# Attention, then a gated network, on one core: 25 instead of 22 visits with both products with V in one block, and a first Strassen pair that no longer waits for the last mask

## The chip, the core and the metric

The kernel runs on one core of a Trainium2 chip. The metric is the time of one execution on the device in microseconds (us), median of three runs. In the texts PE is the matrix engine, DVE the vector engine, ACT the scalar engine, POOL the general engine (GpSimd) and SP the engine that issues the DMAs.

## The reference

Attention over 8 batches, 8 heads, 576 tokens, head size 64, with all scores dropped that lie more than tau = 0.02 under the row's greatest; then a gated network over the 4608 tokens.

```python
scores = scale * q @ k.T                      # (8, 8, 576, 576)
scores = where(scores >= max(scores) - tau, scores, -1e9)
attn = softmax(scores)
x = (attn @ v) as (4608, 512)
out = (sigmoid(x @ w_gate) * (x @ w_val)) @ w_out   # 512 -> 1536 -> 512
```

## The kernel before

**Attention** goes through 32 visits, one for each batch b (0 to 7) and each pair of heads hp (0 to 3); a visit's tiles carry b and hp in their names (`av7_3_0` is of visit (7,3)). A visit has nine tiles of 128 query rows by 576 keys: four for each head, and one (`l`) that holds the 64 left over queries of both. For each tile PE makes scores (`s`, line 669, or 661 in the first four visits), DVE their maximum (676), ACT the exponential (690), DVE the mask with the row sum (693), PE four transposes of the result (`tp`, 770) and one of its left over keys (`lk`, 783), and ACT copies them (`pt`, `pl`). The products with V (`av`, 808) follow for both heads together: each head fills 64 columns of the array, and the two heads stand on different halves of the output's partitions. Two banks of results come of a visit, one for the queries of tiles 0 and 1 and one for tiles 2 and 3 with the left over ones. In an unpaired visit these are two blocks on PE, each placed as soon as its tiles are there. In a paired visit (`PAIRED`) one operation issues both, 68 matmuls in a row. ACT moves both banks to `xf`, POOL multiplies by the reciprocal row sums, which go through DRAM (`rd`, `rb`), and a DMA or a split puts the block away.

**The network** runs over nine blocks of 512 tokens (the ninth gathers the left over ones). Blocks 0 to 2 take three matmuls for each product (high and low halves), as `m` (888), `o` (939) and, for the output of blocks 1 and 2, seven products of a Strassen scheme (`pairp`, 1227). Blocks (3,4), (5,6) and (7,8) go as Strassen pairs: seven products for each piece of the weights, summed in three banks a, b and c (`qa`, `qb`, `qc`, line 1138; then `ra`, `rb`, `rc`, 1284). Bank b lies in a score slot (tag `s`), of which there are two once the network has begun. The operands of the first pair (`xs0_p1` to `xs0_p3`) were put away in DRAM earlier and are loaded into buffers that the attention gives back (`kd`, `k2`, `p`, `vs`, `x`), 512 KB each.

**What sets the order:** a planner goes through all operations with estimated costs, keys and limits on buffers, and fixes one order for each engine. Attention has keys by its tile count, the network's PE work has keys from 1e6 on, so attention goes first wherever it can and the network fills what it leaves. Operations that were ready in the plan but not on the chip hold up what stands behind them on their engine. `masked` is a one-element list: it holds the mask operation that was written last, and at the place where the Strassen pairs are written that is the one of the last tile of visit (7,3). All products of the first pair (`k` = 0) wait for it.

Of the kernel before, what the change touches and what calls it, by code (L numbers as in the profile page):

```python
# [10 lines left out]
F32 = mybir.dt.float32  # L11
F32R = mybir.dt.float32r
I32 = mybir.dt.int32
AF = mybir.ActivationFunctionType
ALU = mybir.AluOpType
# [28 lines left out]
class Plan:  # L44
# [10 lines left out]
    def buf(self, tag, shape, dtype, name, cls=None):  # L55
        return Buf(self, tag, shape, dtype, name, cls)
# [185 lines left out]

NPS = 4

AV_COST, AV_PAIR = 0.0096, 5.25


def PAIRED(b, hp):
    return b >= 3 or b == 2 and hp % 2


def THR(t):
# [59 lines left out]
def act(n):  # L312
    return 0.19 + 0.0008 * n
# [10 lines left out]
def mm(n):  # L324
    return 0.014 + 0.000418 * n
# [3 lines left out]
def kernel(  # L329
# [25 lines left out]
    nc = tc.nc  # L355

    B, NPAIR, _, P, SK = k.shape
# [8 lines left out]
    SM = NJ * P  # L366
# [19 lines left out]
    zero_t = cp.tile([P, 1], F32, tag="zero", name="zero_t")  # L386
# [9 lines left out]
    scale_t = cp.tile([P, 1], F32, tag="scale", name="scale_t")  # L396
# [4 lines left out]
    ps_more = ahead.enter_context(tc.tile_pool(name="ps_more", bufs=1, space=PSUM))  # L401
# [9 lines left out]
    active = {"att": 1, "moe": 0}  # L411

    class Both(Plan):
        def cap(self, tag, cls):
            if tag == "s" and active["moe"]:
                return 2 if cls is None else None
            if tag != "b":
                return None
            if cls == "conv":
                return 1  # L420
            if cls == "att":
                return 2 if active["moe"] else 3
            return 2 if active["att"] else 4
# [19 lines left out]
            if o is last_att[0]:  # L443
                active["att"] = 0

    last_att, first_late, masked, more = [None], [None], [None], [ps_more]
    plan = Both(pools, slots)
    op, buf = plan.op, plan.buf

# [92 lines left out]
    class Visit:  # L542
# [66 lines left out]
        def plain_scores(self, key, n):  # L609

            pair = 4 * self.b + self.hp
# [13 lines left out]
                    ), writes=parts)  # L625
            for h in range(2):
                for j, (c0, c1) in enumerate(pieces if h == 0 else [(0, S)]):
                    op("ACT", act(c1 - c0), key + h, lambda h=h, c0=c0, c1=c1: nc.scalar.activation(
                        qn.ap[:, h, c0:c1], qn.ap[:, h, c0:c1], AF.Copy, scale=scale_t[:, 0:1]
                    ), writes=[(qn, (h, y)) for y in ((j,) if len(pieces) > 1 and h == 0 else (0, 1))])  # L630

    def tile_steps(vis, g, i, key):

# [50 lines left out]
        else:  # L684
# [5 lines left out]
        op("ACT", 0.74, key, lambda: nc.scalar.activation(  # L690
            p(), sv(), AF.Exp, bias=st.ap[:, 0:1], scale=1.0
        ), reads=[s, (st, 0)], writes=[(g.p, i)])
        masked[0] = op("DVE", 0.9, key, lambda: nc.vector.scalar_tensor_tensor(  # L693
            out=p(), in0=sv(), scalar=st.ap[:, 1:2], in1=p(),
            op0=ALU.is_ge, op1=ALU.mult, accum_out=g.sums(i),
        ), reads=[s, (st, 1)], writes=[(g.p, i), g.parts[i]])

    def late_normalise(vis, key):

# [156 lines left out]
    def moe_pe(cost, emit, reads, writes, also=(), after=()):  # L856
        seq[0] += 1
        return op("PE", cost, 1e6 + seq[0] - 1, emit, reads=reads, writes=writes, also=also, after=after)
# [209 lines left out]
    def chains(n, scale, done, tag):  # L1068

        ps_ = {c: buf("s" if c == "b" else "b", [P, SM], F32, f"{tag}{c}{n}", "moe") for c in "abc"}  # L1070
        t = {c: buf("pc" if c == "u3" and not (tag == "r" and n.endswith("_1")) else "t2", [P, SM], F32, f"{tag}{c}{n}") for c in ("p1", "u2", "u3")}

        def plus(bank, x, out):
            if scale == 1.0:
# [27 lines left out]
    def in_two(k, xt, gA, gB):  # L1102

        for f in F1:
            at = {"11": (gA[f], 0), "12": (gA[f], 1), "21": (gB[f], 0), "22": (gB[f], 1)}
            for i in range(2):
# [23 lines left out]
                for prod in SEVEN_IN:  # L1130
# [11 lines left out]

                    also = {"p1": [t["p1"]] + ([gA[f], gB[f]] if i == 0 else []), "p6": [t["u2"]], "p7": [t["u3"]]}.get(prod, [])
                    rd = [(x.b, (x.part, z)) for x in xt[prod] for z in range(2)]
                    end = moe_pe(6 * mm(SM), go, rd + [w], [acc], also=also, after=() if k else masked)
                    after(prod)
                    if prod in ("p6", "p7", "p3"):
                        unit_ends.append(end)
# [9 lines left out]
    def out_pair(g):  # L1158
# [24 lines left out]
            op("SP", 1.0, -1, lambda: nc.sync.dma_start(out=out[row : row + P, col : col + SM], in_=x.ap), reads=[x])  # L1183

        def new(e, n):
            part[e, n] = buf(("rb", "pc")[e] if n == "p7" else "t2", [P, SM], F32, f"{n}pair{e}")
            return part[e, n]

        def after(prod, e, acc):
# [177 lines left out]
    t = 0  # L1367
# [168 lines left out]
```

## Time and profile before

| | |
|---|---|
| median of 3 runs | 1322.38 us (1321.62 to 1323.14) |
| the profiled execution | 1322.47 us |
| its span, first to last instruction | 1320.7 us |
| PE busy | 1301.6 us, 99% of the span |
| DVE, ACT, POOL busy | 71%, 58%, 45% |
| mean granted clock of PE | 0.998 |

The profiled execution is 1.77 us longer than its span; this part lies before the first and behind the last instruction. A busy PE is not a PE at its peak: the profile counts a matmul from its start to a modelled end, and neighbours overlap. So the cost of a piece of PE work is read here from the start of its first matmul to the start of the next piece.

### The profile page before, as it was taken

The numbers are of one execution on the slowest core, as the hardware profiler recorded it, in microseconds if no ns is written. First come the engines' busy times: TensorE is split into PE (matmuls) and PEld (weight loads), VectorE is DVE, ScalarE is ACT, GpSimd is POOL, SyncE is SP. The second block draws the span as 40 slices with busy tenths as digits, with TensorE's granted clock in tenths as the row PEclk, the third lists the DMA queues.
The fourth block names the chain that finished last, engine by engine and source line by source line (L and its number), as shares of the span: only waits on it lengthen the run. The fifth ranks groups of instructions, "written<-read, shape, count | busy, mean of one in ns | idle before, by whom it ended". The sixth has DMA issues, their size and how long they took to land.

```text
span 1320.7 us, 23590 instructions
## 1 busy us (share of the span) xinstructions
PE 1301.6 (99%) x8256; PEld 1074.1 (81%) x8256; DVE 934.7 (71%) x1851; ACT 766.6 (58%) x1409; POOL 598.5 (45%) x527
## 2 busy tenths in 40 slices
PE   8989999999999999999999999999999999999998
PEld 5568888888888888888888888888888888888887
DVE  7889877777777777777777874457945569555594
ACT  7888877777766777777777752223522235222242
POOL 3678878885545547868789830111001100010100
PEclk9999999999999999999999999999999999999999
DMA  7669988888676678898775788666685666756663
GB/s 279 235 209 346 338 261 264 267 267 294 206 249 210 212 244 287 282 309 281 241 223 167 227 303 291 224 189 215 214 284 186 198 201 209 236 192 199 195 208 116
DMA packets 147549, 315.59 MB, mean 239 GB/s; under 512 B 29544, under 2 KB 57448, under 8 KB 147432
## 3 DMA queue, kind: packets, MB, share of 16 engines
q1 hardware_dynamic: 147288, 314.09, 73.2%
q8 instruction: 66, 1.08, 0.3%
q14 instruction: 51, 0.42, 0.1%
q10 hardware_dynamic: 144, 0.00, 0.0%
HBM read 237.34 MB, written 62.01 MB: 227 GB/s over the span
## 4 chain that ended last, share of the span: by engine, by line
PE 94%; DVE 2%; ACT 1%; POOL 1%; issue 1%; DMA 0%; SPq 0%; DVEq 0%; POOLq 0%; ACTq 0%
PE m L888 14%; PE av L808 11%; PE qb L1138 11%; PE s L669 9%; PE tp L770 8%; PE qc L1138 7%; PE qa L1138 7%; PE rb L1284 6%; PE pairp L1227 4%; PE rc L1284 4%; PE ra L1284 4%; PE o L939 3%; PE s_l L669 2%; PE s L661 1%; PE tp_l L770 1%; PE lk L783 1%
## 5 line engine op out<-in xcount | busy, mean ns | idle before, releaser
L676 DVE TENSOR_REDUCE st<-s 128x1 f32<-128x576 f32 x256 | 192.7, 755 | 101.7 <-PE s L669 92.3
L693 DVE SCALAR_TENSOR_TENSOR p<-s,st,p 128x576 f32<-128x576 f32 x256 | 206.5, 812 | 22.4 <-ACT p L690 17.8
L1051 POOL TENSOR_TENSOR gA<-gA 128x512 f32<-128x512 f32 x18 | 24.2, 1346 | 390.2 <-DVE gA L1117 390.2
L690 ACT ACTIVATE p<-s,st 128x576 f32<-128x576 f32 x256 | 190.5, 750 | 10.9 <-DVE st L676 9.6
L726 ACT COPY pt<-tp 128x512 f32<-128x512 f32 x256 | 147.4, 587 | 73.1 <-PE tp L770 69.7
L669 PE MATMUL s<-kd,qd 128*128 128x288 f32 x896 | 165.2, 308 | 0.5 <-DVE p L693 0.4
L888 PE MATMUL m<-x,wi 128*128 128x512 f32 x576 | 158.8, 405 | 0.0
L770 PE MATMUL tp<-ident,p 128*128 128x128 f32 x1024 | 151.2, 274 | 3.2 <-ACT pt L726 1.2
L669 PEld LDWEIGHTS s<-kd,qd 128*128 128x128 f32 x896 | 130.8, 189 | 13.7 <-DVE p L693 4.6
L770 PEld LDWEIGHTS tp<-ident,p 128*128 128x128 f32 x1024 | 121.4, 140 | 23.6 <-issue 4.1
L808 PE MATMUL av<-pt,vs 128*64 128x256 f32 x1024 | 123.5, 383 | 0.7 <-ACT pt L726 0.7
L888 PEld LDWEIGHTS m<-x,wi 128*128 128x128 f32 x576 | 100.2, 189 | 15.1 <-ACT pt L726 0.4
L596 POOL TENSOR_TENSOR kd<-kn,kd 128x640 fp32r<-128x640 f32 x56 | 87.9, 1569 | 53.3 <-ACT kd L594 48.2
L1075 DVE TENSOR_TENSOR qu<-qb,qp 128x512 f32<-128x512 f32 x72 | 49.8, 691 | 84.5 <-PE qb L1138 60.6
L1138 PE MATMUL qa<-xs_p,wa 128*128 128x512 f32 x432 | 109.3, 389 | 0.0
L808 PEld LDWEIGHTS av<-pt,vs 128*64 128x64 f32 x1024 | 69.1, 137 | 38.7 <-issue 5.2
L1138 PEld LDWEIGHTS qa<-xs_p,wa 128*128 128x128 f32 x432 | 81.1, 188 | 16.8
L1043 ACT CAST gs_p<-gA 128x512 fp32r<-128x512 f32 x72 | 43.6, 620 | 85.2 <-DVE gA L1117 53.9
L721 POOL TENSOR_TENSOR xf<-xf,rb 128x576 f32<-128x576 f32 x31 | 44.8, 1445 | 70.1 <-DMA rb<-rd 57.7
L888 PE MATMUL m<-x,ws 128*128 128x512 f32 x288 | 74.8, 401 | 1.4 <-DVE th L914 0.9
L1284 PE MATMUL rb<-gs_p,wo_p 128*128 128x512 f32 x324 | 74.4, 389 | 0.0
L1284 PEld LDWEIGHTS rb<-gs_p,wo_p 128*128 128x128 f32 x324 | 60.8, 188 | 12.6
(149 smaller groups left out, 2679.4 us busy)
## 6 DMA issues: line engine op xcount, KB each, us to landing
kn<-in_k_dram SPq DMA_DIRECT2D x84, 320.0 KB
wi<-wid SPq DMA_DIRECT2D x48, 512.0 KB
wa<-wid SPq DMA_DIRECT2D x36, 512.0 KB
ws<-sid SPq DMA_DIRECT2D x36, 512.0 KB
wt<-sid SPq DMA_DIRECT2D x36, 512.0 KB
wo_p<-sod SPq DMA_DIRECT2D x36, 512.0 KB
qd<-q SPq DMA_DIRECT2D x112, 128.0 KB
wo_p<-wod SPq DMA_DIRECT2D x27, 512.0 KB
```

The source lines that it names most:

```text
L596: op("POOL", pool(SK), key + at, lambda kn=kn, kd=kd: nc.gpsimd.tensor_tensor(out=kd.ap[:, 1, :SK], in0=kn.ap, in1=f32(kd.ap[:, 0, :SK]), ...
L669: nc.tensor.matmul(s.ap[:, c, :HALF], st(), mv(slice(kc + c * HALF, kc + (c + 1) * HALF)), start=m == 0, stop=m == len(steps) - 1,)
L676: op("DVE", 0.76, key, lambda: nc.vector.tensor_reduce(out=st.ap[:, 0:1], in_=sv(), axis=AX.XY, op=ALU.max, negate=True), reads=[s], write ...
L690: op("ACT", 0.74, key, lambda: nc.scalar.activation(p(), sv(), AF.Exp, bias=st.ap[:, 0:1], scale=1.0), reads=[s, (st, 0)], writes=[(g.p, i)])
L693: masked[0] = op("DVE", 0.9, key, lambda: nc.vector.scalar_tensor_tensor(out=p(), in0=sv(), scalar=st.ap[:, 1:2], in1=p(), op0=ALU.is_ge, ...
L726: return op("ACT", act(n), key, lambda: nc.scalar.copy(dst(), src.ap), reads=[src], writes=[part])
L770: nc.tensor.matmul(tp.ap[:, c, :], self.p.ap[:, o + c * P : o + (c + 1) * P], ident, is_transpose=True, start=c == 0, stop=c == NJ - 1, sk ...
L808: nc.tensor.matmul(av.ap[h * D : (h + 1) * D, a:z], vis.vs.ap[:, j, h], m(h), start=i == 0, stop=i == len(ms) - 1, skip_group_check=True,)
L888: nc.tensor.matmul(m.ap, wv[:, a, c * P : (c + 1) * P], xs[c].ap[:, z, c0:c1], start=e == 0, stop=e == 11,)
L1138: nc.tensor.matmul(acc.ap, wv[:, y, (2 * h + c) * P : (2 * h + c + 1) * P], xt[prod][c].get()[:, z], start=e == 0 and prod in FIRST, stop= ...
L1227: nc.tensor.matmul(acc.ap, w.ap[:, e, c, y], gt[prod][2 * h + c].get()[:, z], start=m == 0 and h == 0, stop=m == 5 and h == NFG - 1,)
L1284: nc.tensor.matmul(acc.ap, w.ap[:, e, c, y], gt[prod][2 * g + c].get()[:, z], start=m == 0 and g == 0 and prod in FIRST, stop=m == 5 and g ...
```

## The change

1. `PAIRED` holds for three more visits: (1,3), (2,0) and (2,2). That makes 25 paired visits.
2. The first Strassen pair's products don't wait for the last mask any more. The bank b of a Strassen sum may take one score slot, not two, as long as attention runs (`cap`).
3. `masked` is now a list of all nine masks of visit (7,3). The sums of tokens that DVE makes for the Strassen schemes still wait for them.
4. Two buffers move: the third partial sum of the first pair's input products (`u3`) goes from the single `pc` to the shared `t2`, and a partial sum of `out_pair` from `pc` to `qn`.
5. `Q_POOL` is an empty tuple, so the new branch that it opens is never taken.

```diff
 def PAIRED(b, hp):
-    return b >= 3 or b == 2 and hp % 2
+    return b >= 2 or b == 1 and hp == 3
...
             if tag == "s" and active["moe"]:
-                return 2 if cls is None else None
+                return 2 if cls is None else 1 if active["att"] else None
...
-        masked[0] = op("DVE", 0.9, key, lambda: nc.vector.scalar_tensor_tensor(
+        mask = op("DVE", 0.9, key, lambda: nc.vector.scalar_tensor_tensor(
...
+        if (vis.b, vis.hp) == (B - 1, NPAIR - 1):
+            masked.append(mask)
...
-        t = {c: buf("pc" if c == "u3" and not (tag == "r" and n.endswith("_1")) else "t2", [P, SM], F32, f"{tag}{c}{n}") for c in ("p1", "u2", "u3")}
+        t = {c: buf("pc" if c == "u3" and not (tag == "r" and n.endswith("_1") or tag + n[0] == "q0") else "t2", [P, SM], F32, f"{tag}{c}{n}") for c in ("p1", "u2", "u3")}
...
-                    end = moe_pe(6 * mm(SM), go, rd + [w], [acc], also=also, after=() if k else masked)
+                    end = moe_pe(6 * mm(SM), go, rd + [w], [acc], also=also)
...
-            part[e, n] = buf(("rb", "pc")[e] if n == "p7" else "t2", [P, SM], F32, f"{n}pair{e}")
+            part[e, n] = buf(("rb", "qn")[e] if n == "p7" else "t2", [P, SM], F32, f"{n}pair{e}")
```

Since the planner goes through everything again, each engine's order changes from visit (1,3) on until the second group of products of the first Strassen pair. What stands ahead of that and behind it is in the same order as before.

PE at visit (1,3), before: the end of the first block `av1_3_0`, what stands between, and the start of the second block `av1_3_2`.

```order
L808 MATMUL av1_3_0_2968<-pl1_3_00_2736,vs1_3_1798 64x128
L808 MATMUL av1_3_0_2968<-pl1_3_10_2954,vs1_3_1798 64x128
L770 MATMUL tp1_3_121_2995<-ident_71,p1_3_12_2917 128x128 x4
L669 MATMUL s2_0_001_3003<-kd2_0_0_2516,qd2_0_0_2668 128x288 x4
L783 MATMUL lk1_3_12_3011<-ident_71,p1_3_12_2917 128x128
L669 MATMUL s2_0_l40_3015<-k22_0_2704,q22_0_2635 128x288 x6
L808 MATMUL av1_3_2_3027<-pt1_3_02_2847,vs1_3_1798 64x256
```

The same place on PE now: what stands ahead of the first block, and the border between the two.

```order
L781 MATMUL tp1_3_121_2984<-ident_71,p1_3_12_2917 128x128 x4
L794 MATMUL lk1_3_12_2994<-ident_71,p1_3_12_2917 128x128
L678 MATMUL s2_0_001_2996<-kd2_0_0_2516,qd2_0_0_2668 128x288 x4
L950 MATMUL o0_0_3005<-g0_0_1497,wo0_0_0_2749 128x512 x3
...
L678 MATMUL s2_0_l40_3026<-k22_0_2704,q22_0_2635 128x288 x6
...
L819 MATMUL av1_3_0_3044<-pt1_3_00_2684,vs1_3_1798 64x256
...
L819 MATMUL av1_3_0_3044<-pl1_3_10_2954,vs1_3_1798 64x128
L819 MATMUL av1_3_2_3057<-pt1_3_02_2847,vs1_3_1798 64x256
```

The last transposes of the visit, which stood between the blocks, and 14 matmuls of the network, which followed the second block, now stand ahead of the first, and the second block follows it at once. The orders of the whole kernel have 42 separate stretches of `av` on PE before and 39 now.

POOL in the same stretch of the program, before: the low halves of two visits' keys (`kd`, line 596) among the sums of weights (`s0_o`, `s1_o`) and the tokens of block 1 (`x1`).

```order
L840 TENSOR_TENSOR x1_2_3142<-xf1_2_2601,x1_2_3142 128x512
L920 TENSOR_TENSOR g0_11_3166<-th0_11_0_2929,g0_11_3166 128x512
L596 TENSOR_TENSOR kd2_1_1_3157<-kn2_1_1_2988,kd2_1_1_3157 128x640
L721 TENSOR_TENSOR xf1_3_3001<-xf1_3_3001,rb1_3_3112 128x576
L990 TENSOR_TENSOR s0_o1_0_3052<-s1_o1_0_3140 128x2x128
```

POOL there now:

```order
L1001 TENSOR_TENSOR s1_o1_0_3150<-wo0_2_1_2922 128x4x128
L1001 TENSOR_TENSOR s0_o1_0_3126<-s1_o1_0_3150 128x2x128
L598 TENSOR_TENSOR kd2_1_1_3169<-kn2_1_1_2981,kd2_1_1_3169 128x640
L1001 TENSOR_TENSOR s0_o1_0_3126<-s0_o1_0_3126 128x2x128
L1001 TENSOR_TENSOR s1_o1_0_3150<-s0_o1_0_3126,s1_o1_0_3150 128x2x128
L732 TENSOR_TENSOR xf1_3_3109<-xf1_3_3109,rb1_3_3121 128x576
```

The keys `kd2_1_1` and the normalisation of visit (1,3) stand a few places further back, behind more sums of weights; the tokens `x1_2` have moved ahead.

PE at the end of attention, before: the last output product of blocks 1 and 2 (`pairp3_1`), then the first products of the first Strassen pair around the scores of the last left over tile (`s7_3_l40`). Four products later the block `av7_3` follows.

```order
L1227 MATMUL pairp3_1_10909<-gpp3_5_10899,wpair_p3_2_10605 128x512 x3
L1138 MATMUL qa0_0_0_10959<-xs0_p1_0_10546,wa20_0_0_10615 128x512 x3
L1138 MATMUL qa0_0_0_10959<-xs0_p1_1_10683,wa20_0_0_10615 128x512 x3
L669 MATMUL s7_3_l40_10971<-k27_3_10335,q27_3_10322 128x288 x6
L1138 MATMUL qb0_0_0_10984<-xs0_p6_0_10757,ws20_0_0_10655 128x512 x3
```

PE there now: the last transposes of visit (7,3), its `av` block, and further down the start of the first Strassen pair.

```order
L781 MATMUL tp7_3_121_10893<-ident_71,p7_3_12_10827 128x128 x4
L794 MATMUL lk7_3_12_10900<-ident_71,p7_3_12_10827 128x128
L1238 MATMUL pairp4_0_10761<-gpp4_5_10766,wpair_p4_2_10461 128x512 x2
L1238 MATMUL pairp4_1_10809<-gpp4_4_10759,wpair_p4_2_10461 128x512 x2
L819 MATMUL av7_3_0_10912<-pt7_3_00_10659,vs7_3_9949 64x256
...
L1238 MATMUL pairp3_1_10978<-gpp3_5_10972,wpair_p3_2_10705 128x512 x3
L1149 MATMUL qa0_0_0_11027<-xs0_p1_0_10501,wa20_0_0_10716 128x512 x3
L1149 MATMUL qa0_0_0_11027<-xs0_p1_1_10737,wa20_0_0_10716 128x512 x3
L1149 MATMUL qb0_0_0_11039<-xs0_p6_0_10798,ws20_0_0_10725 128x512 x3
L1149 MATMUL qb0_0_0_11039<-xs0_p6_1_10852,ws20_0_0_10725 128x512 x3
L1149 MATMUL qc0_0_0_11056<-xs0_p5_0_10862,ws20_0_0_10725 128x512 x3
```

The left over tile of visit (7,3) has moved far ahead (it now follows `av7_2`), and all of attention's PE work stands ahead of the first Strassen product, where five of these products stood among its pieces before.

## Rows read from the trace of the kernel before

**Rows 1.** The page: busy time and share of the span of each engine, the two lines of forty slices for PE and its granted clock, and the chain of work that ended last by engine.

```profile
PE 1301.6 (99%) x8256; PEld 1074.1 (81%) x8256; DVE 934.7 (71%) x1851; ACT 766.6 (58%) x1409; POOL 598.5 (45%) x527
PE   8989999999999999999999999999999999999998
PEclk9999999999999999999999999999999999999999
PE 94%; DVE 2%; ACT 1%; POOL 1%; issue 1%; DMA 0%; SPq 0%; DVEq 0%; POOLq 0%; ACTq 0%
```

**Rows 2.** Busy time of each engine in seven stretches of the span (from:to in us, then us busy and instructions of PE, its weight loads, DVE, ACT, POOL, then PE's granted clock, the share of the DMA engines and GB/s).

```profile
0.00:110.00 110.00, 96.39 (x732) 66.52 (x733) 90.39 (x190) 90.84 (x173) 67.17 (x95) 0.98 0.75 257
110.00:210.00 100.00, 98.57 (x674) 81.23 (x674) 85.68 (x173) 81.33 (x153) 79.89 (x68) 1.00 0.92 309
210.00:310.00 100.00, 99.96 (x786) 84.76 (x786) 73.99 (x172) 76.93 (x147) 82.95 (x74) 1.00 0.80 263
310.00:800.00 490.00, 489.76 (x3746) 414.50 (x3743) 358.00 (x828) 355.62 (x664) 317.03 (x253) 1.00 0.77 250
800.00:830.00 30.00, 30.00 (x181) 24.28 (x180) 14.99 (x25) 6.19 (x11) 5.59 (x4) 1.00 0.79 261
830.00:1310.00 480.00, 480.00 (x2119) 397.40 (x2119) 310.26 (x466) 155.69 (x264) 45.90 (x34) 1.00 0.65 207
1310.00:1320.70 10.70, 6.90 (x31) 5.38 (x29) 1.38 (x2) 0.00 (x0) 0.00 (x0) 0.92 0.21 74
```

**Rows 3.** Timeline of PE at visit (1,3), unpaired (start in us, us, line, what, how many).

```profile
210.96 0.71 PE L888 MATMUL m<-x,ws 128*128 128x512 f32 x2
211.60 1.95 PE L808 MATMUL av<-pt,vs 128*64 128x256 f32 x16
213.38 0.61 PE L808 MATMUL av<-pl,vs 128*64 128x128 f32 x8
213.91 0.66 PE L770 MATMUL tp<-ident,p 128*128 128x128 f32 x4
214.33 0.78 PE L669 MATMUL s<-kd,qd 128*128 128x288 f32 x4
...
215.93 1.95 PE L808 MATMUL av<-pt,vs 128*64 128x256 f32 x16
...
218.83 0.66 PE L770 MATMUL tp<-ident,p 128*128 128x128 f32 x4
```

**Rows 4.** Timeline of PE at a paired visit.

```profile
322.41 0.60 PE L770 MATMUL tp<-ident,p 128*128 128x128 f32 x4
322.76 1.64 PE L888 MATMUL m<-x,wi 128*128 128x512 f32 x6
...
325.25 0.72 PE L888 MATMUL m<-x,wi 128*128 128x512 f32 x2
325.80 0.69 PE L669 MATMUL s<-kd,qd 128*128 128x288 f32 x4
...
330.59 1.95 PE L808 MATMUL av<-pt,vs 128*64 128x256 f32 x16
...
335.65 0.79 PE L669 MATMUL s<-kd,qd 128*128 128x288 f32 x4
336.28 1.04 PE L770 MATMUL tp<-ident,p 128*128 128x128 f32 x8
```

**Rows 5.** The chain of work that ended last, in order of time, its longest pieces: the first and the last of the 22 paired `av` blocks in it, which have 68 matmuls each.

```profile
260.36 5.06 PE av L808 x68
...
804.31 5.06 PE av L808 x68
```

**Rows 6.** Timeline of all engines at the end of attention: PE's work, the two copies of the last `av` block by ACT, and an issue of loads of the first Strassen pair's operands.

```profile
797.33 0.95 PE L669 MATMUL s_l<-k,q 128*128 128x288 f32 x6
803.10 0.80 SPq L1338 DMA_DIRECT2D xs_p<-xsd_p  x2
804.24 1.49 PEld L808 LDWEIGHTS av<-pt,vs 128*64 128x64 f32 x16 [0.35 <-issue]
806.67 0.37 ACT L726 COPY xf<-av 128x256 f32<-128x256 f32 x1 [3.17 <-PE av L808]
809.42 0.43 ACT L726 COPY xf<-av 128x320 f32<-128x320 f32 x1 [2.37 <-PE av L808]
814.88 2.88 PE L1138 MATMUL qc<-xs_p,ws 128*128 128x512 f32 x12
```

**Rows 7.** The same columns as in rows 2, for stretches around the start of the first Strassen pair.

```profile
780.00:790.00 10.00, 10.00 (x54) 8.44 (x53) 7.33 (x16) 5.78 (x10) 2.60 (x3) 1.00 0.98 332
790.00:800.00 10.00, 10.00 (x49) 8.38 (x48) 3.03 (x6) 1.85 (x3) 0.00 (x0) 1.00 1.03 386
810.00:820.00 10.00, 10.00 (x46) 8.27 (x45) 4.15 (x6) 2.60 (x5) 0.00 (x0) 1.00 0.56 176
```

**Rows 8.** Groups of instructions by line over the whole span (busy us, mean ns of one, idle time of the engine just before them and what ended it).

```profile
L888 PE MATMUL m<-x,wi 128*128 128x512 f32 x576 | 158.8, 405 | 0.0
L596 POOL TENSOR_TENSOR kd<-kn,kd 128x640 fp32r<-128x640 f32 x56 | 87.9, 1569 | 53.3 <-ACT kd L594 48.2 <-DMA vs<-in_v_dram 4.5 <-PE pairp L1227 0.3
L1138 PE MATMUL qa<-xs_p,wa 128*128 128x512 f32 x432 | 109.3, 389 | 0.0
L1227 PE MATMUL pairp<-gpp,wpair_p 128*128 128x512 f32 x252 | 66.5, 402 | 0.0
L939 PE MATMUL o<-g,wo 128*128 128x512 f32 x144 | 38.2, 403 | 0.0
```

More of the change, by code (lines that the diff above doesn't have):

```diff
@@ L243 @@
 NPS = 4
+Q_POOL = ()
 AV_COST, AV_PAIR = 0.0096, 5.25
 def PAIRED(b, hp):
-    return b >= 3 or b == 2 and hp % 2
+    return b >= 2 or b == 1 and hp == 3
 def THR(t):
@@ L444, in started @@
                 active["att"] = 0
-    last_att, first_late, masked, more = [None], [None], [None], [ps_more]
+    last_att, first_late, masked, more = [None], [None], [], [ps_more]
     plan = Both(pools, slots)
@@ L627, in plain_scores @@
                 for j, (c0, c1) in enumerate(pieces if h == 0 else [(0, S)]):
-                    op("ACT", act(c1 - c0), key + h, lambda h=h, c0=c0, c1=c1: nc.scalar.activation(
-                        qn.ap[:, h, c0:c1], qn.ap[:, h, c0:c1], AF.Copy, scale=scale_t[:, 0:1]
-                    ), writes=[(qn, (h, y)) for y in ((j,) if len(pieces) > 1 and h == 0 else (0, 1))])
+                    dst = [(qn, (h, y)) for y in ((j,) if len(pieces) > 1 and h == 0 else (0, 1))]
+                    if pair not in Q_POOL:
+                        op("ACT", act(c1 - c0), key + h, lambda h=h, c0=c0, c1=c1: nc.scalar.activation(
+                            qn.ap[:, h, c0:c1], qn.ap[:, h, c0:c1], AF.Copy, scale=scale_t[:, 0:1]
+                        ), writes=dst)
+                        continue
+                    op("POOL", 0.83, key + h, lambda h=h, c0=c0, c1=c1: nc.gpsimd.tensor_scalar(
+                        out=qn.ap[:, h, c0:c1], in0=qn.ap[:, h, c0:c1], scalar1=scale_t[:, 0:1], scalar2=zero_t[:, 0:1],
+                        op0=ALU.mult, op1=ALU.add,
+                    ), writes=dst)
     def tile_steps(vis, g, i, key):
```

## The prediction

> **What bounds the kernel now.** I read the page first. PE is busy 99% of the span, every slice from the fourth to the last but one is at nine tenths or more, the granted clock is at the upper of the two levels (2.4 GHz), and the chain of work that ended last runs 94% over PE [rows 1]. The share of busy time hides where PE still waits, so I read the stretches next [rows 2]. The first 110 us lose 13.6 us (110.00 - 96.39) and the next 100 us lose 1.4 us. From 210 to 1310 us PE is idle for 0.04 + 0.24 + 0.00 + 0.00 us, and at the end it stops about 3.8 us before the span does. The order of the changed kernel is the same as before ahead of visit (1,3), whose first `av` block starts at 211.60 us [rows 3], and the same again soon after the first Strassen pair has begun, near 830 us. So the change acts on a stretch in which PE is the bound and has almost nothing to wait for. There only two things count: how much PE work there is, and whether a new wait appears.
>
> **The change part by part.** *Three more paired visits.* No matmul is added or taken away. What goes is one border for each visit between an `av` block, in which each instruction fills 64 columns, and the full-width work around it. I price it from starts. At visit (1,3) the first block takes 213.91 - 211.60 = 2.31 us and the second 218.83 - 215.93 = 2.90 us [rows 3], in sum 5.21. A paired block takes 335.65 - 330.59 = 5.06 us [rows 4], and it does so at both ends of the row of 22 such blocks [rows 5]. Inside the blocks that is 0.15 us less. Going in costs too: two `m` matmuls take 0.64 us when `av` follows (210.96 to 211.60) [rows 3] and 0.55 us when scores follow (325.25 to 325.80) [rows 4], so 0.09 us. And coming out: four transposes take 0.42 us behind an `av` block (213.91 to 214.33) [rows 3] and 0.35 us elsewhere (322.41 to 322.76) [rows 4], so 0.07 us. One border is worth 0.15 + 0.09 + 0.07 = 0.31 us, three of them 0.93 us. The low end is the part inside the blocks alone, 3 x 0.15 = 0.45 us. For the high end I add 0.02 us of reading error to each of the two small terms: 3 x 0.35 = 1.05 us. I take 0.93, since all three parts lie on PE, which has no idle time there to swallow them.
>
> *What the pairing moves.* The last transposes of the three visits and some network matmuls move ahead of the block. On PE that only swaps neighbours. The copies by ACT, the mask work by DVE and the normalisation by POOL move with them; from 210 to 310 us these engines are busy 77%, 74% and 83% [rows 2], so there is room, least on POOL. I put this at nothing, covered by the network's matmuls between the tiles; what it costs without that cover is the first and the last rival.
>
> A paired block also leaves two banks to be copied at once. The two copies of such a block by ACT took 0.37 and 0.43 us [rows 6], together 0.80 us, and yet the scores behind a block started without a pause [rows 4]. The Trainium skill (TensorEngine Tiling (Array Packing), section "PSUM Bottleneck") says that packing small matmuls speeds up the matrix engine but not the emptying of its banks, so that the copies may become the bound, and this speaks against longer packed blocks. By that rule the three blocks would each wait for both copies, 3 x 0.80 = 2.40 us, and the time would be 1323.9 us, still no measurable difference. By the trace the rule does not bite here, as the 5.06 us are the same in [rows 5], and I leave it out of the sum.
>
> *The early start of the Strassen pair.* The words of the change promise an overlap, but the new order doesn't have it: on PE the first product `qa0_0_0` now stands behind the last `av` block, where before five products stood ahead of it. What the removed wait does is let the planner place the left over tile of visit (7,3) early, with the rest of its visit. Before, its scores ran at 797.33 us [rows 6], among the Strassen products. PE was busy without a gap from 780 to 800 us [rows 7] and in the whole stretch from 800 to 830 us [rows 2], so there is no idle time to win. The one small pause that the trace shows there is 0.35 us in front of the last `av` block's weight loads [rows 6], and a pause of that kind can also stand in the new order, where only four matmuls separate the last `lk` from the block. I take zero, with 0.35 us to either side.
>
> *Loads.* The operands of the third product (`p5`) are now needed as third and not as tenth. Its second operand was among the loads issued at 803.10 us and was used at 814.88 us [rows 6]. It goes into a buffer that the left over tile holds, and that tile is now done early, so its load moves forward too: in the order of SP it stands behind `xs0_p7_0`, where it was the last of the fourteen. Zero, with the price of a late load among the rivals.
>
> *Buffers and the unused branch.* `u3` in `t2` and a partial sum in `qn` change who waits in the plan, not what is computed. Behind 830 us the orders agree, and there PE has 480.00 of 480.00 us [rows 2]. `Q_POOL` is empty. Both cost nothing; a cost below zero is excluded for the same reason, as no idle time is there to be won.
>
> The sum: 1322.47 - 0.93 = 1321.54 us for the profiled execution. The median of the runs lies 0.09 us below the profiled time, so 1321.5 us.
>
> **The rivals.** *Slower: POOL falls behind in the newly paired stretch.* Of all engines beside PE, POOL is the fullest there, 82.95 of 100 us [rows 2], and the new order puts the low halves of the keys (`kd2_1_1`) behind more sums of weights. One such instruction takes 1.57 us [rows 8]. If each of the three visits kept PE waiting for one of them, that would be 3 x 1.57 = 4.71 us and 1322.47 - 0.93 + 4.71 = 1326.3 us. It decides from 2.6 + 0.9 = 3.5 us of waiting on. For it: the order is fixed for each engine, so one late instruction holds up everything behind it, and from 110 to 210 us, with POOL at 79.89 and DVE at 85.68 us of 100, PE did lose 1.4 us [rows 2]. Against it: POOL was idle for 53.3 us in front of these instructions, 48.2 us of it waiting for ACT's half [rows 8], so it waits for its inputs more than they for it; and from 210 to 310 us PE lost 0.04 us with POOL as full as that. Chance 0.11.
>
> *Faster: hidden waits go.* Network matmuls among attention's tiles have means of 405, 402 and 403 ns, the same shape in the Strassen stretch 389 ns [rows 8]. Over 576, 252 and 144 of them that is 9.2 + 3.3 + 2.0 = 14.5 us. If these were short waits that a better order removes, a quarter of them would be 3.6 us, and the time 1317.9 us. Against it: four transposes that take 0.60 us are followed 0.35 us after their start by the next matmul [rows 4], so the first matmul behind transposes is recorded too early and too long. Most of the 14.5 us is that, not waiting. Chance 0.06.
>
> *Late loads.* From 780 to 800 us the DMA engines are full, with shares of 0.98 and 1.03 [rows 7]. If the two operands of `p5` came late by their own transfer, 2 x 512 KB at the 386 GB/s of that stretch [rows 7], that is 2 x 1.36 = 2.7 us and 1324.3 us. Against it: from 810 to 820 us the share is 0.56, so the pile is short. Chance 0.05.
>
> *The pairing wins nothing.* A paired block can't start before its two banks are free, and if each new block waits the 0.35 us that the last one shows [rows 6], 3 x 0.35 = 1.05 us takes back the 0.93: 1322.6 us. Against it: blocks such as that at 330.59 us [rows 4] show no wait. Chance 0.08.
>
> **How the numbers follow.** The forecast has the rest, 0.70. About 0.2% (2.6 us) is what a measurement of this kernel can tell from no change, so faster means under 1319.7 and slower over 1325.0 us. The forecast, late loads and the lost gain all lie within: 0.70 + 0.05 + 0.08 = 0.83. Faster 0.06, slower 0.11. The range runs from 1319.8 us (the forecast with the larger border price and 1.5 us of hidden waits gone) to 1325.0 us (late loads, and 0.7 us for the spread of single runs); outside it are the first two rivals, 0.17.
>
> **What would show it.** In the changed profile there should be 25 `av` blocks of 68 matmuls, each of 5.06 us from its start to the next, at (1,3), (2,0) and (2,2) too; PE idle by less than half a microsecond from 210 to 800 us; no Strassen product ahead of the last `av` block; `qa`, `qb` and `qc` without a gap from the first on. It is wrong if PE's matmuls of scores wait for POOL between 210 and 310 us, if the first Strassen products have gaps that end with a landing, or if the means of `m`, `o` and `pairp` fall toward 389 ns.

## The result and the profile after

The change makes the kernel slower: 1332.88 us at the median of 5 runs (1325.66 to 1335.28), against 1322.38 us of before in 5 runs on the same chip. The ratio is 1.0061 with a 95% interval of 1.0035 to 1.0087. The profiled execution took 1333.98 us; its span is 1332.1 us.

The stretches of [rows 2] in the changed kernel, with the same columns:

```profile
110.00:210.00 100.00, 98.59 (x676) 81.26 (x674) 85.73 (x173) 81.38 (x154) 79.96 (x68) 1.00 0.91 305
210.00:310.00 100.00, 100.00 (x776) 85.10 (x776) 72.47 (x171) 76.88 (x147) 84.59 (x76) 1.00 0.86 272
310.00:800.00 490.00, 480.60 (x3707) 406.98 (x3708) 361.82 (x824) 352.94 (x659) 316.05 (x252) 0.99 0.74 238
800.00:830.00 30.00, 30.00 (x179) 24.49 (x176) 11.71 (x19) 6.11 (x11) 1.43 (x1) 1.00 0.93 324
830.00:1310.00 480.00, 480.00 (x2120) 397.44 (x2119) 311.53 (x468) 155.15 (x263) 49.97 (x37) 1.00 0.66 212
```

For PE four of the five are as before. From 310 to 800 us PE now loses 9.40 us (490.00 - 480.60) where it lost 0.24. PE's waits from 210 to 830 us (what waited for what: us in total, times, longest):

```profile
PE s L678 <- DVE p_l L702: 8.2, 1, 8.2
PE s L678 <- DVE p L702: 1.1, 1, 1.1
```

Two single waits make up the loss. The large one is in visit (7,1). DVE's timeline there (start, us, line, what):

```profile
688.40 0.75 DVE L685 TENSOR_REDUCE st_l<-s_l 128x1 f32<-128x576 f32 x1
689.18 10.32 DVE L586 SCALAR_TENSOR_TENSOR q<-qn,scale_t,q 128x640 fp32r<-128x640 f32 x1
699.42 0.81 DVE L702 SCALAR_TENSOR_TENSOR p<-s,st,p 128x576 f32<-128x576 f32 x1
700.47 0.82 DVE L702 SCALAR_TENSOR_TENSOR p_l<-s_l,st_l,p_l 128x576 f32<-128x576 f32 x1
```

One instruction, the **low half of q** of the visit (`scale * qn - high half`, both inputs in SBUF), stood for 10.32 us. There are 28 of them, and their median is 0.91 us. Two masks are queued behind it, and PE's next scores need the bank that the second one frees. POOL in the same time, and PE:

```profile
687.44 2.53 POOL L1057 TENSOR_TENSOR gpp<-g,gpp 128x512 fp32r<-128x512 f32 x2
689.93 2.50 POOL L1062 TENSOR_TENSOR g<-g 128x512 f32<-128x512 f32 x2
692.40 1.53 POOL L598 TENSOR_TENSOR k<-kn,k 128x640 fp32r<-128x640 f32 x1
693.90 2.48 POOL L1057 TENSOR_TENSOR gpp<-g,gpp 128x512 fp32r<-128x512 f32 x2
696.34 2.48 POOL L1062 TENSOR_TENSOR g<-g,g 128x512 f32<-128x512 f32 x2
```
```profile
693.00 0.29 PE L819 MATMUL av<-pl_l,vs 128*64 128x64 f32 x4
701.44 1.30 PE L678 MATMUL s<-kd,qd 128*128 128x288 f32 x4 [8.15 <-DVE p_l L702]
702.53 1.91 PE L781 MATMUL tp<-ident,p 128*128 128x128 f32 x8
```

Each POOL instruction follows the one before it without a gap, up to 698.82 us (696.34 + 2.48). DVE's instruction ends 0.68 us behind that, at 699.50. In the kernel before, the same instruction met POOL's sums too, but took 1.23 us, and there it was a POOL instruction that gave way (two took 3.12 us where two take about 2.50):

```profile
695.21 1.23 DVE L584 SCALAR_TENSOR_TENSOR q<-qn,scale_t,q 128x640 fp32r<-128x640 f32 x1
```
```profile
694.46 3.12 POOL L1051 TENSOR_TENSOR g<-g,g 128x512 f32<-128x512 f32 x2
```

PE then ran slowly: `s x4` took 1.30 us (0.69 elsewhere). The granted clock (next to last but one column) was 0.50 behind the wait, the lower level of 1.2 GHz, and 1.00 (2.4 GHz) again from 708 us on:

```profile
701.40:705.00 3.60, 3.56 (x16) 3.58 (x17) 0.97 (x2) 1.11 (x3) 0.00 (x0) 0.50 0.89 282
705.00:707.00 2.00, 2.00 (x10) 1.68 (x9) 1.56 (x3) 1.20 (x3) 0.00 (x0) 0.50 0.90 190
707.00:708.00 1.00, 1.00 (x6) 0.81 (x5) 0.13 (x2) 0.74 (x3) 0.00 (x0) 0.69 0.83 188
```

That is 0.50 x 5.6 + 0.31 x 1.0 = 3.11 us of lost work. The small wait is at 491 us. There PE does scores, transposes and scores again with no network matmul between, and DVE is busy almost without a break with the maxima and masks that free the banks:

```profile
488.67 0.77 PE L678 MATMUL s<-kd,qd 128*128 128x288 f32 x4
489.48 0.66 PE L781 MATMUL tp<-ident,p 128*128 128x128 f32 x4
491.27 0.80 PE L678 MATMUL s<-kd,qd 128*128 128x288 f32 x4 [1.14 <-DVE p L702]
```

The account: 1322.47 - 0.93 (the three borders, as forecast) + 8.15 + 3.11 + 1.14 = 1333.94 us, against 1333.98.

The loss can also be read between two places that all these kernels share: the second `av` block of visit (1,2), ahead of everything that moved, and the first product `ra`, behind it. The first two lines are of the kernel before, the other two of the changed one:

```profile
188.42 1.95 PE L808 MATMUL av<-pt,vs 128*64 128x256 f32 x16
914.18 2.88 PE L1284 MATMUL ra<-gs_p,wo_p 128*128 128x512 f32 x12
188.41 1.95 PE L819 MATMUL av<-pt,vs 128*64 128x256 f32 x16
925.55 2.88 PE L1295 MATMUL ra<-gs_p,wo_p 128*128 128x512 f32 x12
```

From the one to the other it took 725.76 us before and 737.14 us after, 11.38 us more.

### The profile page after: what moved, and what is told of

It is laid out like the page before. It is cut to its first block, busy times and chain, and to the rows that moved or that the text cites. A ratio compares the mean times of both kernels' runs of the same rounds, so it can differ in the third digit from the quotient of the medians.

```text
span 1332.1 us, 23597 instructions
## 1 busy us (share of the span) xinstructions
PE 1303.7 (98%) x8256; PEld 1076.2 (81%) x8256; DVE 940.9 (71%) x1851; ACT 765.9 (57%) x1409; POOL 599.3 (45%) x527
## 4 chain that ended last, share of the span: by engine, by line
PE 94%; DVE 2%; issue 2%; ACT 1%; DMA 1%; POOL 0%; SPq 0%; DVEq 0%; ACTq 0%; POOLq 0%
PE m L899 14%; PE av L819 11%; PE qb L1149 11%; PE s L678 9%; PE tp L781 8%; PE qa L1149 7%; PE qc L1149 7%; PE rb L1295 6%; PE pairp L1238 4%; PE rc L1295 4%; PE ra L1295 4%; PE o L950 2%; PE s_l L678 2%; PE s L670 1%; PE tp_l L781 1%
```

## The experiments

My theory (A in the texts below): POOL kept the low half of q waiting, because its instructions followed each other without a pause. Rivals: the DVE instruction is slow by itself; or the three paired visits, or the early Strassen start, cost by their places. As the time of one kernel scatters, the table also counts runs over 1327.5 us, 5 us above the usual time of before. The kernel before has such runs too, 15 of 98 beside all these kernels.

| kernel | median us (runs) | over 1327.5 us | ratio to before, 95% interval |
|---|---|---|---|
| after | 1332.88 (5) | 4 | 1.0061, 1.0035 to 1.0087 |
| e1 pairing alone | 1325.22 (10) | 3 | 1.0026, 0.9996 to 1.0057 |
| e2 all but the pairing | 1323.42 (10) | 3 | 1.0019, 1.0002 to 1.0035 |
| e3 low half of (7,1) on POOL | 1331.84 (4) | 4 | 1.0071, 1.0056 to 1.0086 |
| e4 POOL pauses once, in (7,1) | 1326.79 (6) | 3 | 1.0036, 1.0021 to 1.0052 |
| e5 after, 12 pauses | 1325.55 (11) | 0 | 1.0012, 1.0001 to 1.0023 |
| e6 before, 12 pauses | 1322.67 (11) | 0 | 0.9990, 0.9974 to 1.0005 |
| e7 after, 4 pauses | 1323.90 (12) | 0 | 1.0000, 0.9985 to 1.0015 |
| e8 pairing alone, 4 pauses | 1323.34 (12) | 0 | 0.9995, 0.9981 to 1.0010 |
| e9 all but the pairing, 4 pauses | 1322.13 (12) | 0 | 0.9977, 0.9959 to 0.9995 |
| e10 after, one-column instructions | 1326.82 (12) | 4 | 1.0023, 1.0008 to 1.0038 |
| e11 e2 with these | 1323.47 (12) | 0 | 0.9997, 0.9985 to 1.0010 |

**e1, the pairing alone.** The kernel before with `PAIRED` of after, and one of the change's two buffer moves.

```diff
-    return b >= 3 or b == 2 and hp % 2
+    return b >= 2 or b == 1 and hp == 3
...
-            part[e, n] = buf(("rb", "pc")[e] if n == "p7" else "t2", ...
+            part[e, n] = buf(("rb", "qn")[e] if n == "p7" else "t2", ...
```

> The kernel before with the 25 paired visits and one buffer moved (the partial sum p7 of the second pair goes into qn); cap, u3 and the wait on the mask work stay as before. Theory A (POOL's row): the loss of the changed kernel is one DVE instruction of visit (7,1), the low half of q, that stood 10.32 us beside an unbroken row of POOL instructions; it depends on how POOL's instructions fall around that one, so this kernel, whose order of POOL in visit (7,1) is another, should be free of it: 1321.5 to 1323.0 us, PE idle under 1 us from 310 to 800 us. Theory B (the pairing itself costs, through the three blocks): the loss is there, 1330 to 1334 us, with the wait near the three visits or in (7,1) again. Theory C (what is at fault is the earlier Strassen start, which lets network work be spread otherwise): none of the loss, so this run alone doesn't part A and C, the next does.

Its profiled run (1332.98 us) has the wait in (7,1) again, 8.0 us, and the 1.1 us near 491 us. But most other runs are near 1324 us. So my guess that another order of POOL would be free of it failed (POOL's row there is the same as in after), and the cost isn't in the three blocks, which run as forecast in the same trace.

**e2, all but the pairing.** The changed kernel with `PAIRED` of before.

> The changed kernel with the 22 paired visits of before; all the rest of the change is in. Theory A (POOL's row): depends on the order around the low half of q in visit (7,1); if POOL's instructions there fall otherwise, 1322.0 to 1323.5 us. Theory B (the pairing itself costs): 1322.0 to 1323.5 us. Theory C (the earlier start of the Strassen pair is at fault): 1330 to 1334 us with a wait of PE scores for DVE in visit (7,1) or near it.

Its profiled run (1330.62 us) has a low half of 8.06 us at 695.99 us, in (7,1) again, behind other POOL instructions, and no wait near 491 us. So the long wait belongs to neither half of the change, and the 1.1 us belong to the pairing.

**e3, the low half on POOL**, in (7,1) only:

```diff
-                nc.vector.scalar_tensor_tensor(out=q2.ap[:, 1], in0=qn.ap, scalar=..., in1=f32(q2.ap[:, 0]), ...)
+                nc.gpsimd.tensor_scalar(out=qn.ap, in0=qn.ap, scalar1=scale_t[:, 0:1], ...)
+                nc.gpsimd.tensor_tensor(out=q2.ap[:, 1], in0=qn.ap, in1=f32(q2.ap[:, 0]), op=ALU.subtract)
```

> The changed kernel, except that the low half of q of visit (7,1), one DVE instruction, is made by two POOL instructions in the same place of the order. Theory A (DVE is kept out by POOL's row): with no DVE instruction with two inputs from SBUF in that place the 8.15 us of PE's wait and the 3 us at half clock behind it are gone, and POOL has 2 to 3 us more: 1321.5 to 1324.0 us. Rival D (the half of q is late because its input or POOL's work is late, whoever makes it): PE waits there again, 1330 to 1335 us. Rival E (another instruction of DVE behind it was the slow one): 1330 to 1335 us too, with the next DVE instruction of the chain stretched.

A miss in the time. (7,1) was free of its wait, but the next visit's low half took its place, behind a row of POOL instructions that was now longer:

```profile
720.07 7.93 DVE L588 SCALAR_TENSOR_TENSOR q<-qn,scale_t,q 128x640 fp32r<-128x640 f32 x1
```

**e4, POOL pauses.** A one-column POOL instruction reads DVE's result, so POOL waits for it:

```diff
+                if (b, hp) == (7, 1):
+                    nc.gpsimd.tensor_scalar(out=pad_t[:, 0:1], in0=f32(q2.ap[:, 1, 0:1]), ...)
```

> The changed kernel plus one POOL instruction of one column that reads the low half of q of visit (7,1), placed in POOL's order behind the sum that runs when DVE's instruction begins; POOL so pauses until DVE is done. Theory A (DVE gets no turn while POOL's instructions follow each other without a pause): the DVE instruction takes 0.9 to 3.5 us (up to the end of one POOL instruction) and not 10.32, PE waits under 1.5 us there, 1321.5 to 1324.0 us. Rival F (the DVE instruction is slow by itself, by its data or by a transfer): it takes 10 us still, POOL waits behind it, 1331 to 1336 us.

In (7,1) the low half took 1.38 us (690.02) in place of 10.32: it ends when POOL pauses, so it isn't slow by itself. The one of (7,2) took 4.06 us, PE waited 1.3 us for it, and the median stayed above the forecast.

**e5 and e6, pauses in all late visits**, with `if b >= 5` in e4's edit, on the changed kernel and on the one before:

> The changed kernel plus the one-column POOL instruction of the previous kernel, now behind the low half of q in every visit from (5,0) on (12 visits), so that POOL pauses for each of them until DVE is done. Theory A (DVE is kept out while POOL's instructions follow each other without a pause, by chance in one late visit or another): no low half of q over 2.2 us from 500 us on, PE waits of 1.1 us near 491 us (the order's own) and under 1 us elsewhere, and the highest of the runs falls with the median: median 1322 to 1324 us, none over 1326. Rival G (POOL's pauses are repaid by lateness of POOL's own work): single waits for POOL appear, 1325 to 1330 us. Rival F (the long DVE instruction is not POOL's doing): a low half of 8 to 10 us appears again, 1330 us.

> The kernel before plus the same one-column POOL instruction behind the low half of q in every visit from (5,0) on. Theory A: the kernel before already runs at about 1322.5 us with rare runs near 1331 (2 of 21 so far), so the median stays, 1322 to 1323 us, and runs over 1326 us no longer occur. Rival G (pauses of POOL cost): 1324 to 1328 us. If the rare slow runs of before come from something else, they occur here as well (about 1 of 10).

No low half over 1.82 us from 500 us on in either, and no run over 1327.1 us. e6 met its forecast. e5 misses its own in the median and in the highest run: its profile has new waits of 1.5 us (transposes of PE for ACT) and 0.9 us (`pairp` for POOL). I put them down to the pauses of POOL, so rival G was right in part.

**m1, the dispute by itself.** Rows of 12 POOL instructions, and one DVE instruction that asks early in the row, with both inputs in SBUF or one in a bank:

```python
for j in range(12):
    nc.gpsimd.tensor_tensor(out=outs[j], in0=a, in1=c, op=ALU.subtract)   # one of four kinds
nc.vector.scalar_tensor_tensor(out=lo, in0=qn, scalar=scale_t, in1=hi, ...)   # or in0=bank
```

> A kernel that leaves the reference's whole computation out: 60 trials, in each a row of 12 POOL instructions on 128 x 512 elements and one DVE instruction of the form of the low half of q that asks while the row runs, at six different phases. Rows of POOL: two inputs from SBUF with outputs apart, the same in place, the same each reading the last one's result, and one input from SBUF. DVE: both inputs from SBUF, or one of them from a bank. Theory A (kept out by an unbroken row): with two SBUF inputs some of the DVE instructions beside a row of two-input POOL instructions last several of them, up to the rest of the row (12 x 1.25 = 15 us), the others end at the first end of a POOL instruction (1 to 2.2 us); with one input from a bank none takes longer than 1.5 us. Rival F: all take about 0.9 to 2.2 us whatever POOL does, and what made the instruction of visit (7,1) long is something else.

The 48 with two SBUF inputs (L94) and the 12 with one in a bank (L97), min/median/max in ns:

```profile
L94 DVE SCALAR_TENSOR_TENSOR lo<-qn,scale,hi x48: 751/1208/1793, 14.6 to 716.6; 128x512 f32<-128x512 f32 x48
```
```profile
L97 DVE SCALAR_TENSOR_TENSOR lo<-bank,scale,hi x12: 750/751/752, 723.5 to 896.6; 128x512 f32<-128x512 f32 x12
```

With an input from a bank nothing is paid. (These 12 asked behind at most five POOL instructions; the 256 masks of the changed kernel, which have one input in a bank, took 774 to 821 ns beside all its rows.) With two from SBUF DVE waits for the end of the running POOL instruction, and no longer than 1.79 us. All of them asked behind seven instructions or fewer. So "a row keeps DVE out" was not the whole theory.

**e7, e8, e9, pauses in the last batch only** (`if b == 7`), on after, e1 and e2:

> The changed kernel with the one-column POOL instruction behind the low half of q in the four visits of the last batch only ((7,0) to (7,3)). Theory A with the order's own 1.1 us wait near 491 us, and nothing else lost: 1322.47 - 0.93 + 1.14 + at most 0.7 for POOL's pauses = 1322.7 to 1323.4 us at the median, no run over 1326. If what is left of the loss of 12 guards (1325.55 us) is not POOL's pauses but something in the new order besides the wait near 491 us: 1325 to 1326 us again. If other visits than those of the last batch are kept out as well: single runs over 1327 us.

> The kernel before with the 25 paired visits and p7 in qn, and the POOL instruction behind the low half of q in the last batch's visits. It gives the price of the pairing without DVE's being kept out: by the prediction's border term and the wait near 491 us, -0.93 + 1.14 = +0.2 us on before, 1322.3 to 1323.3 us, no run over 1326; if the pairing costs more by its places, 1324 us or more.

> The changed kernel with the 22 paired visits of before and the same guard in the last batch's visits. It gives the price of the rest of the change without DVE's being kept out: the prediction's zero for the early start, 1322.0 to 1323.0 us, no run over 1326. If the early start costs by itself, 1324 us or more.

e8 and e9 came as forecast (e8 0.04 us above its range), e7 0.5 us above its range, with 0.8 us of waits of `pairp` for POOL in its profile. In 36 runs none is over 1325.1 us. The ratios of these three are to runs of before of which 7 of 29 were over 1327.5 us. Beside the other 22, whose median is 1322.88 us, e7 is 1.02 us slower, e8 0.46 us slower and e9 0.75 us faster, so freed of the long wait the whole change still costs about 1 us, and the gain of e9 is small. The traces agree. Between the two places named above it took 725.76 us before, and these are the two lines of e8:

```profile
187.59 1.95 PE L814 MATMUL av<-pt,vs 128*64 128x256 f32 x16
913.53 2.88 PE L1290 MATMUL ra<-gs_p,wo_p 128*128 128x512 f32 x12
```

That is 725.94 us, 0.18 more, with the wait of 1.14 us near 491 us in it. So the pairing by itself gained 0.96 us there. e9 took 725.30 us (187.47 to 912.77) and e7 727.14 (189.30 to 916.44). e6, which only adds pauses to before, took 725.54 (188.48 to 914.02), so 0.2 us is not to be read out of one trace.

**m2, company.** 216 asks in an unbroken row, one to every third POOL instruction, alone and beside ACT, PE and loads.

> A kernel that leaves the reference's whole computation out: an unbroken row of POOL instructions with two inputs from SBUF (3 for each ask) and 36 DVE instructions of the form of the low half of q in each of six stretches: nothing beside them; ACT writes the high half just ahead of each; ACT also copies banks; TensorE also runs matmuls; loads from memory also run; loads alone. In the measured row without company no DVE instruction was kept out longer than one POOL instruction. If company decides (another engine's or the loads' traffic in SBUF), DVE instructions of over 2.2 us appear in the stretches with that company and not in the first; if what decides is the wait for ACT's half, from the second stretch on; if none of these, all 216 stay under 2.2 us and what decides stays open.

```profile
L106 DVE SCALAR_TENSOR_TENSOR lo<-qn,scale,hi x216: 874/1067/2003, 25.0 to 869.4; 128x640 fp32r<-128x640 f32 x108
```

None was kept out, so company alone doesn't do it. But as DVE had a turn at every third POOL instruction, this run can't say what company does behind a long row. (The loads ran ahead, so they kept company with the first stretch, at a share of 1.04, and not with the fifth and sixth.)

**m3, the row's length.** In the traces so far the kept-out instructions stood behind rows of 11, 11, 11, 22 and 23 POOL instructions without a pause (a gap of 0.08 us or more counted as one).

```python
for j in range(28):
    nc.gpsimd.tensor_tensor(out=outs[j % 12], in0=a, in1=c, op=ALU.subtract)
# ACT's chain of copies (or DVE's of bank reductions) times the one ask
nc.vector.scalar_tensor_tensor(out=lo, in0=qn, scalar=scale_t, in1=hi, ...)
```

> A kernel that leaves the reference's whole computation out. Every low half of q that was kept out so far stood behind POOL rows of 11, 11, 11, 22 and 23 instructions without a pause, and the some 60 that were let in at the first end of a POOL instruction behind rows of 1 to 7 (one behind 11). In the two measuring kernels so far the row was short, or DVE's last turn was less than three POOL instructions ago. Here each trial is a row of 28 POOL instructions with two inputs from SBUF, and DVE's one instruction with two inputs from SBUF asks behind 1 to 20 of them. Theory H (a long row without a turn of DVE keeps DVE out for its rest): asks behind some number on, near 8 to 11, last up to the row's end (28 - 11 = 17 POOL instructions, about 21 us), those behind fewer end at the first end of a POOL instruction (1 to 2 us). Theory K (the row's length does not matter): all of the 60 asks without a guard are under 2.2 us. Ten asks in which POOL's row has a one-column instruction that reads DVE's result: 1 to 3 us by both.

Asks behind 11, 12, 14 and 23 instructions, and behind 23 with a pause:

```profile
309.18 1.01 DVE L90 SCALAR_TENSOR_TENSOR lo<-qn,scale,hi 128x512 f32<-128x512 f32 x1 [12.59 <-ACT hi L80]
345.94 20.42 DVE L90 SCALAR_TENSOR_TENSOR lo<-qn,scale,hi 128x512 f32<-128x512 f32 x1 [13.91 <-ACT hi L80]
419.44 17.80 DVE L90 SCALAR_TENSOR_TENSOR lo<-qn,scale,hi 128x512 f32<-128x512 f32 x1 [16.56 <-ACT hi L80]
713.66 7.25 DVE L90 SCALAR_TENSOR_TENSOR lo<-qn,scale,hi 128x512 f32<-128x512 f32 x1 [27.14 <-ACT hi L80]
2489.65 1.18 DVE L90 SCALAR_TENSOR_TENSOR lo<-qn,scale,hi 128x512 f32<-128x512 f32 x1 [27.14 <-ACT hi L80]
```

This is theory H, with a limit somewhat higher than I expected. Of the 60 asks without a pause 31 took at most 1.79 us, one end of a POOL instruction or two, and 29 lasted to the row's end. Up to 11 instructions all were let in, from 15 on all were kept out, between them either happened. PE and loads had no part in it.

**m4, what the limit counts and what sets it back.**

> A kernel that leaves the reference's whole computation out. Four kinds of rows of POOL, DVE's ask at rising places in them. Half (48 instructions on 256 columns, about 0.74 us each): if the limit counts instructions (12 to 15), asks behind 15 of them (about 11 us) and more last to the row's end; if it counts time (15 to 18 us), it takes 20 to 25 instructions. Single (28 instructions with one SBUF input, about 0.8 us): if only rows with two inputs keep DVE out, none is over 1.5 us; if any row does, those behind 12 to 15 instructions last to the end. Column (rows of two-input instructions with a one-column instruction behind every fourth): if a short instruction sets the limit back, none is over 3 us; if not, those behind 12 to 15 last to the end. Turn (DVE has one turn some 6 instructions into the row, then asks again): if a turn sets the limit back, the second ask is kept out only from 12 to 15 instructions behind the turn on; if not, from 6 to 9 behind it.

| row | let in behind | kept out behind |
|---|---|---|
| 256 columns, two inputs | 14 instructions (9.1 us) and fewer | 18 (11.7 us) and more, to the row's end |
| one input | 13 (9.1 us) and fewer | 14 (10.4 us) to 23, until behind the 24th or 25th of 28 |
| a one-column instruction behind every fourth | 9 | 10 and more, until the next one-column instruction, at most 5.56 us |
| DVE had a turn behind 7 | up to 21, 13 behind its turn | none |

The limit isn't a time alone: 10.4 us were too long in one row here, and 15.7 us not in a row of m3. The number of instructions fits the first two rows and m3, which all lie between 12 and 18. It doesn't fit the third, where 10 were enough, two of them one-column instructions. So what is counted stays open. The second row shows that DVE isn't always kept out to the end: this ask got in while the row (441.98 to 463.60 us) still had 2.7 us to go, and why is open.

```profile
452.36 8.51 DVE L77 SCALAR_TENSOR_TENSOR lo<-qn,scale,hi 128x512 f32<-128x512 f32 x1 [9.94 <-ACT hi L76]
```

One input in SBUF is enough for POOL. A turn of DVE sets the limit back; a one-column instruction doesn't, but lets DVE in. An ask behind 10 instructions in the third kind, and what POOL did:

```profile
668.50 0.34 POOL L93 TENSOR_SCALAR red<-zero 128x1 f32<-128x1 f32 x1
668.74 5.56 DVE L77 SCALAR_TENSOR_TENSOR lo<-qn,scale,hi 128x512 f32<-128x512 f32 x1 [9.94 <-ACT hi L76]
668.80 4.92 POOL L91 TENSOR_TENSOR pout<-pa,pc 128x512 f32<-128x512 f32 x4
673.71 0.81 POOL L93 TENSOR_SCALAR red<-zero 128x1 f32<-128x1 f32 x1
```

**e10 and e11, such openings in the kernel**, with no wait for DVE, on after and e2:

```diff
+                if e == "POOL" and next(turns) % 2:
+                    nc.gpsimd.tensor_scalar(out=pad_t[:, 0:1], in0=zero_t[:, 0:1], ...)
```

> The changed kernel with a one-column POOL instruction, which reads nothing that changes, behind every second of POOL's sums for the Strassen stage (34 of them), and no guard. If DVE is let in at such an instruction as in the measuring kernel: the low halves of the last batch take at most 5 us (four POOL instructions), mostly under 3, PE waits at most 2 to 3 us in place of 8.15, the clock stays at the upper level, median 1323 to 1326 us, no run over 1329. If only POOL's waiting for DVE helps: 8 to 10 us again in most runs, 1330 to 1335 us.

> The changed kernel with the 22 paired visits of before and the same one-column instructions. If they open POOL's rows: no long runs (3 of 10 were long without them), median 1321.5 to 1323.5 us, as with the guard (1322.13). If not: single runs near 1330 us.

e10's low half of (7,1) was let in at the one-column instruction, as in m4:

```profile
691.23 2.51 POOL L1065 TENSOR_TENSOR g<-g 128x512 f32<-128x512 f32 x2
693.73 0.96 POOL L1067 TENSOR_SCALAR pad<-zero_t 128x1 f32<-128x1 f32 x1
```
```profile
690.46 4.02 DVE L586 SCALAR_TENSOR_TENSOR q<-qn,scale_t,q 128x640 fp32r<-128x640 f32 x1
```

The two long ones of its profile are 4.02 and 5.19 us and cost PE 3.2 us together, at a clock of 1.00. Its median is 0.8 us above the range that I gave, and one run of 1330.12 us above its limit, so an opening behind every second sum may come too seldom. e11 met its forecast, but lies 1.3 us above e9, the same kernel with four pauses instead, which ran on another chip.

## Why the prediction was wrong

**What bounds the kernel** was right: only a new wait could cost anything, and two did, one of them with a lower clock behind it.

**Three borders, 0.93 us:** the blocks came as forecast, 68 matmuls and 5.06 us at 217.11, 240.34 and 286.70 us, and the account closes to 0.04 us with it. Between the two shared places after has 11.38 - 8.15 - 3.11 - 1.14 = -1.02 us left for it, and e8 -0.96 us. The times of the runs, with their scatter, can't show so small a gain.

**"I put this at nothing, covered by the network's matmuls":** this is the step that failed. What the reordering moves was not at nothing in two places, both outside the stretch from 210 to 310 us for which I had read the engines' shares. Near 491 us the new order has no network matmul between three scores, and PE waits 1.14 us; every kernel here with 25 paired visits has this wait in its profile, none with 22. It takes back the 0.93. And in (7,1) DVE was kept out by POOL, which cost PE 8.15 us and 3.11 us of clock. This one isn't the pairing's alone, as e2 has it too. That the shares of busy time left room said nothing, since DVE lost its turn, not its time: e7, with the same work and four pauses of POOL, has no run over 1325.1 us. The share of POOL from 310 to 800 us (317.03 of 490.00) also hid the place. In the kernel before POOL (the fifth pair of numbers) was busy 39.00 of 40 us around visit (7,1):

```profile
680.00:720.00 40.00, 40.00 (x296) 33.74 (x296) 29.93 (x72) 33.37 (x60) 39.00 (x31) 1.00 0.61 184
```

**The first rival** named POOL, but with another place and mechanism: from 210 to 310 us PE has 100.00 of 100 us, and PE never waits for POOL's keys. It had the price of one POOL instruction (1.57 us) for each visit. In (7,1) the price was the rest of POOL's row.

**What was at the limit already.** The kernel before had a row of 11 in (7,1) too, and its low half got in. 15 of its 98 runs were over 1327.5 us, none of e6's 11, which fits being kept out now and then. It isn't shown: no such run of before was traced, and at 15 of 98 eleven runs without one come up about once in six by chance. In m3 every ask behind 11 was let in, and the limit lay just above. In the kernels, whose rows mix shapes, three asks behind 11 were kept out (after, e1, e2) and one was let in (before). So a row of 11 is near the limit, and I take it for a matter of chance. Why the chance is 4 of 5 in after and 3 of 10 in e1, with the same eleven instructions, stays open.

**Copies of two banks, early start, loads, buffers:** right. No block is followed by a wait for ACT, no Strassen product stands ahead of the last `av` block, 800 to 830 and 830 to 1310 us have no gap, and e9 shows that all but the pairing costs nothing. The 0.35 us that I took for a possible pause of PE in front of the last block was idle time of the weight loads; PE was busy for all 30.00 us there. **Hidden waits** didn't go: the means of `m`, `o` and `pairp` are 404, 404 and 403 ns over all their matmuls, far from the 389 of the Strassen stretch.

**The Trainium skill** (SBUF — State Buffer, "Who interferes with whom") says that a DVE instruction with two SBUF inputs contends with a GpSimd instruction that reads SBUF, and that one with at most one, outside DVE's two-port modes, doesn't. m1 agrees: up to 1.79 us for the one, at most 0.752 us for the other. Its "Summary: rules for kernel authors" has the second one to issue blocked until the first finishes. Behind short rows that is what m1 and m2 show; behind long ones DVE was kept out over 16 further instructions in m3 (20.42 us), and there the measurement decides.

## What to carry to other kernels

Where DVE and POOL work side by side, read the rows of POOL's instructions without a pause, not its share: a DVE instruction with two inputs in SBUF that asks behind some ten of them may have to wait for the row's end, or nearly. Break such a row where DVE must get in, by a POOL instruction that waits for DVE's result (cheap where POOL has slack) or by one-column instructions. A move that swaps work between equal engines on paper is not free until the order shows what still covers each wait, in the whole stretch that the planner can reorder.

## What the runs showed of the hardware

- POOL can keep a DVE instruction with two inputs in SBUF out over many instructions: 20.42 us in m3 for an instruction that took 0.751 us at the least in m1. It takes a row of POOL instructions without a pause: 12 to 18 of them in rows of one kind, 11 in the kernels, 10 in the row with one-column instructions. A turn of DVE starts it anew (m4). What is counted, and what in the chip makes it, is open.
- A DVE instruction with one input in a bank isn't kept out: 774 to 821 ns for all 256 masks of after.
- After 8.15 us of waiting PE ran at the 1.2 GHz level for 5.6 us, which added 3.11 us. Behind the 5.3 us of e3 the clock was 0.50 as well; the waits of 1.14 us in after and of up to 1.8 us in e10 left it at 1.00.
